# Cross attention and an MLP on one core: the second slot reordered, a transpose three steps later, the last tile's column halves in two banks

## The chip, the cores and the metric

The kernel runs on one core of a Trainium2 chip. The metric is the device time of one execution in microseconds (us), as the median of several runs. Five engines take part: TensorE (PE in the profile, with its weight loads as PEld), VectorE (DVE), ScalarE (ACT), GpSimd (POOL) and SyncE (SP), which here issues DMAs only.

## The reference, cut to what matters

There are B = 8 batches, H = 8 heads, S = 512 rows, 32 state rows and D = 64. Softmax attention runs both ways between `x` and `state`, the results of a batch are laid out as 544 rows of 512 values, and all rows go through an MLP with exact GELU and 2048 inner columns.

```python
a = softmax(scale * x @ state.T);   xread = a @ state      # 512 rows of a head
a2 = softmax(scale * state @ x.T);  sread = a2 @ x         # 32 rows of a head
rows = concatenate([xread, sread])                         # heads side by side: [B * 544, 512]
h = rows @ w_in
out = (0.5 * h * (1 + erf(h / sqrt(2)))) @ w_out           # float32
```

## The kernel before

The work is staged by batch. For a batch `b`:

- `xtr_dma` (L269) transposes its `x` by DMA into `xT`, after `rearr` (L214) on POOL has put it in order. `scores` (L316, once for each half) multiplies on PE and takes the exponent on ACT. `norm` (L338) sums, inverts and multiplies on DVE into `a`. `atr_dma` (L364) transposes `a` by DMA into `AT`, from SP's queue.
- `pmat` or `p_run` (L429, L798) makes P, the product of the state with `w_in`, in four chunks of 512 columns. A chunk takes eight small matmuls into two banks of PSUM and one copy each by ACT and DVE (`p_copy`). P lets the read-out and the first layer of the MLP be one product.
- `M(k)` is the first layer: with `k = 16 * b + m` it multiplies `P` by `AT` for the m-th 128 inner columns (L478, two matmuls) and takes the GELU on ACT (L485). Two of them, a pair, make one step of a slot.
- `U(u)` is a quarter of the second layer for one block of rows in batches 0 and 1 (`mm2`, L504, four matmuls). From batch 2 on the second layer is instead done with seven products of half-size blocks (Strassen's scheme in Winograd-like form): `g_sum` forms sums of GELU blocks on DVE (L580), `X(b, name)` multiplies them (L586) and combines the results on DVE, ACT and POOL (L605, L608, L635, L641, L643). `w_sums(i)` forms the sums of weights that this needs, on DVE (L552). `load_x` on POOL fetches a later batch, held back by a tiny copy named `hold` that waits for a GELU.
- `sread(b)` multiplies for the 32 state rows, `sread_out` normalises them, and `srt(b)` (L399) transposes them on PE into a bank of PSUM, from where DVE copies them into `XSR` (L405). `XSR` is read in the last slot only, by `mm1_sr` (L518), which handles the state rows of all batches.

The order of each engine's work is written out by hand: the schedule is manual, and each engine executes its instructions in the order in which the program issues them. A slot is the stretch with the `M` of one batch, in eight steps p = 0 to 7. The slots of batches 2 to 7 are one loop (L948), in which `X` and `g_sum` of the batch before, `scores`, `norm`, `atr_dma`, `srt` and the P chunks of the next batch have their steps. The second slot, of batch 1, is written out at its beginning (M(16) to M(19)) and is then a loop over p = 2 to 7 (L923).

PSUM has eight banks here: four with the tag `f`, which `ftile` gives out in turn to `M`, `scores`, `pmat`, `sread` and `srt`, and four with tags `o0` to `o3`, which `otile` gives out by name or in turn to the second layer and to some chunks of P. A tile in a bank can be written again only when its reader is done.

The last batch has its own tail: `L4`, `L5`, `L2`, `L1`, `L7`. `L1` and `L7` sum two products into the same bank, one after the other, for the two row blocks `j` of 128 rows and NH = 256 columns. The result of `L1` is read out with an add (L693) before `L7` adds its own product and is read with another add (L717). For j = 1 `L7` goes by column halves of 128, both in one tile, and the last DMA is issued from ACT.

Of the kernel before, what the change touches and what calls it, by code (L numbers as in the profile page):

```python
# [17 lines left out]
def kernel(  # L18
# [36 lines left out]
    def otile(shape, name, at=None):  # L55
        if at is None:
            at = turn[0] % 4
            turn[0] += 1
        return ps_o.tile(shape, FP32, name=name, tag=f"o{at}")
# [256 lines left out]
    def scores(b, half):  # L316
        A = atts[b]
        if half == 0:
            begin_e(b)
        pt = ps_f.tile([128, SJ, 2, 2, NS], FP32, name="pt", tag="f")  # L320
        for ci in range(2):
            c = 2 * half + ci
            for j in range(SJ):
                nc.tensor.matmul(  # L324
                    pt[:, j, :, ci, :],
                    lhsT=A.xT[:, j, c, :],
                    rhs=sbd[:, b, c, :],
                    start=True,
                    stop=True,
                )  # L330
        nc.scalar.activation(  # L331
            out=A.e[:, :, 64 * half:64 * half + 64],
            in_=pt.rearrange("p j t c n -> p (j t) (c n)"),
            func=AF.Exp,
            scale=scale,
        )

    def norm(b, half):  # L338
        A = atts[b]
        G = SJ * 2  # L340
        hs = slice(64 * half, 64 * half + 64)
        e4 = A.e[:, :, hs].rearrange("p g (c n) -> p g c n", n=NS)
        cs = att.tile([128, G, 2], FP32, name="cs", tag="cs")
        nc.vector.reduce_sum(out=cs, in_=e4, axis=AX.X)  # L344
        ics = att.tile([128, G, 2], FP32, name="ics", tag="ics")
        nc.vector.reciprocal(out=ics, in_=cs)
        nc.vector.tensor_tensor(  # L347
            out=A.a[:, :, hs].rearrange("p g (c n) -> p g c n", n=NS),
            in0=e4,
            in1=ics[:, :, :].to_broadcast((128, G, 2, NS)),  # L350
            op=ALU.mult,
        )
# [11 lines left out]
    def atr_dma(b):  # L364
        A = atts[b]
        A.AT = att.tile([128, SJ, 2, 128], BF16, name="AT", tag="AT")
        nc.sync.dma_start_transpose(
            out=A.AT.rearrange("p j t n -> p (j t) n"), in_=A.a
        )
# [59 lines left out]
    def pmat(b, f):  # L429
        p_copy(b, f, p_mm(b, f, ftile))  # L430
# [152 lines left out]
    def x_mm(ps, lhs, rhs, first, js=(0, 1)):  # L583
        for j in js:
            for m in range(MH):
                nc.tensor.matmul(  # L586
                    ps[:, j - js[0], :],
                    lhsT=lhs[:, m, 128 * j:128 * j + 128],
                    rhs=rhs[:, m, :],
                    start=(first and j == js[0] and m == 0),  # L590
                    stop=(m == MH - 1),
                    skip_group_check=True,
                )
# [54 lines left out]
    def rows_out(h, js, ns, eng):  # L648
        b = B - 1
        rows = out[b * SB:b * SB + S, :].rearrange("(p j) n -> p j n", j=SJ)  # L650
        eng.dma_start(
            out=rows[:, 2 * h + js.start:2 * h + js.stop, ns], in_=xs[b, "o", h][:, js, ns]
        )
# [25 lines left out]
    def L2():  # L679
# [5 lines left out]
        xs[b, "v"] = c_tile("v")  # L685
        nc.vector.tensor_tensor(out=xs[b, "v"], in0=xs[b, "y"], in1=c21, op=ALU.subtract)

    def L1():
        b = B - 1
        for j in range(2):  # L690
            ps = xs[b, "x", j] = otile([128, 1, NH], "xp", 2 - 2 * j)
            x_mm(ps, xs[b, "g1"], w_sum["1"], True, (j,))
            nc.vector.tensor_tensor(  # L693
                out=xs[b, "o", 1][:, j, right],
                in0=ps[:, 0, :],
                in1=xs[b, "v"][:, j, :],
                op=ALU.add,
            )
        rows_out(1, both, right, nc.sync)

    def L7():
        b = B - 1
        o = xs[b, "o", 0]
        h = NH // 2
        for j, pieces in ((0, ((0, NH),)), (1, ((0, h), (h, NH)))):
            ps = xs[b, "x", j]
            for n0, n1 in pieces:
                for m in range(MH):
                    nc.tensor.matmul(
                        ps[:, 0, n0:n1],  # L710
                        lhsT=xs[b, "g7"][:, m, 128 * j:128 * j + 128],
                        rhs=w_sum["7"][:, m, n0:n1],
                        start=False,
                        stop=(m == MH - 1),
                        skip_group_check=True,
                    )
                nc.vector.tensor_tensor(  # L717
                    out=o[:, j, n0:n1],
                    in0=ps[:, 0, n0:n1],
                    in1=xs[b, "u"][:, j, n0:n1],  # L720
                    op=ALU.add,
                )
                eng = nc.scalar if j and n0 else nc.sync
                rows_out(0, slice(j, j + 1), slice(n0, n1), eng)

    rs = {}

# [80 lines left out]
    def M(*ms):  # L808
        for m in ms:
            mm1(m // MC, m % MC)  # L810
# [109 lines left out]
    U(16)  # L920


    u = 17  # L923
    for p in range(2, 8):
        if p == 4:
            scores(2, 0)
            scores(2, 1)
            norm(2, 0)
            norm(2, 1)
        if p == 7:  # L930
            atr_dma(2)
        if p == 3:
            begin(3)
            rearr(3)
            xtr_dma(3)
            rearr_ones(3)
        M(16 + 2 * p, 17 + 2 * p)
        U(u)
        u += 1
        if p in (5, 7):  # L940
            pmat(2, 2 + p // 7)
        if p >= 3:
            w_sums(p - 3)
        if p == 2:
            nc.gpsimd.tensor_copy(out=hold, in_=gs[1][:, 4, 0:1])
            load_x(4)

    for b in range(2, B):  # L948
        nb = b + 1
        for p in range(8):  # L950
            k = 16 * b + 2 * p
            if p == 1 and nb < B:
                scores(nb, 0)
                scores(nb, 1)
            if p in (2, 3) and nb < B:
                norm(nb, p - 2)
            if p == 3 and nb + 1 < B:
                xtr_dma(nb + 1)
            if p == 5 and nb < B:
                atr_dma(nb)  # L960
            if p == 3 and nb < B:
                srt(b)
            if p == 7 and nb == B - 1:
                srt(nb)
            M(k, k + 1)
            if b == 2:
                for _ in range(2 if p < 4 else 1):
                    if u < 32:
                        U(u)
                        u += 1  # L970
            elif p < 5:
                if p == 0:
                    g_sum(b - 1, "5")
                X(b - 1, "45127"[p])
                if p < 3:
                    g_sum(b - 1, "127"[p])
            if nb == B and p < 4:
                for m in range(4 * p, 4 * p + 4):
                    mm1_sr(m)
            if p == 1 and nb < B:  # L980
                sread(b)
                sread_out(b)
            if p == 4 and nb == B - 1:
                sread(nb)
                sread_out(nb)
            if p == 0 and b + 3 < B:
                nc.gpsimd.tensor_copy(out=hold, in_=gs[b][:, 0, 0:1])  # L987
                load_x(b + 3)
            if p == 0 and nb + 1 < B:
                begin(nb + 1)  # L990
                rearr(nb + 1)
            if p == 2 and nb + 1 < B:
                rearr_ones(nb + 1)
            if nb == B:
                if p == 4:
                    r_homes()
                    r_sum("5")
                    r_sum("2")
                if p == 5:
                    g_sum(b, "6")  # L1000
                    R("3")
                    r_sum("1")
                    R("4")
                    r_sum("6")
                    r_sum("7")
                if p == 6:
                    R("5")
                    X(b, "3")
                    R("2")
                    R("1")  # L1010
                if p == 7:
                    R("6")
                    X(b, "6")
                continue
            if p == 5:
                g_sum(b, "6")
                if nb < B:
                    p_run(nb, (0, 1), ((0, 1), (3, 2)))
            if p == 6:
                X(b, "3")  # L1020
            if p == 7:
                if nb < B:
                    p_run(nb, (2, 3), ((1, 2), None))
                X(b, "6")
# [41 lines left out]
```

The softmax here doesn't subtract the row's maximum and nothing guards it: scores larger than these inputs give would overflow.

## Time and profile before

| What | Value |
|---|---|
| Median of 11 runs | 209.74 us (209.39 to 211.74) |
| The profiled execution | 209.43 us, span 207.7 us |
| Granted clock of TensorE | 0.997 |
| Busy in the span: PE, DVE, ACT, POOL | 97%, 66%, 64%, 30% |
| Second slot from M(20) to the first M of batch 2 | from 41.63 to 54.82 us |
| First matmul of `L7` | from 202.26 us |

The span reaches from the first instruction of the profile to the last; the profiled execution's own time is 1.7 us longer. Rows of a timeline give the start, the length, the engine, the line, the operation and its tiles, and in brackets how long the engine was idle before and what released it. Rows of waits give the engine and line that waited, what for, the total in us, how often, and the longest. The ends of matmuls are modelled, so stretches of PE's work are best taken from start to start. Starts below are in us from the beginning of the span.

### The profile page before, as it was taken

What the parts mean: (1) busy time and instruction counts of PE and PEld (TensorE: products, weight loads), DVE (VectorE), ACT (ScalarE), POOL (GpSimd) and SP (SyncE); (2) the same over time, 40 slices, a digit from 0 to 9 for tenths busy, and PEclk for the clock granted to TensorE, in tenths of its full rate; (3) what the DMA queues carried; (4) which work ended last, traced back from release to release, by engine and by line L of the source; (5) the groups of instructions that cost most, each with busy time, mean ns of one, the idle gap of its engine ahead of it and who ended that gap; (6) DMA issues with size and microseconds to landing.
All of it is one profiled execution on the core that took longest, in us unless ns stands there. A gap on an engine that the chain in (4) does not pass through costs nothing.

```text
span 207.7 us, 4699 instructions
## 1 busy us (share of the span) xinstructions
PE 200.9 (97%) x1971; PEld 131.1 (63%) x1971; DVE 137.9 (66%) x218; ACT 133.2 (64%) x240; POOL 62.4 (30%) x69
## 2 busy tenths in 40 slices
PE   7799999998999999999999999999999999999993
PEld 7545444453454577756775677667775787778882
DVE  2954675748929649994699658855887553165872
ACT  3864866679794779565956787587757576744120
POOL 8964402573171015710577005500220001200000
PEclk9999999999999999999999999999999999999998
DMA  6999999789384908736681505360106001030224
GB/s 197 198 183 204 206 193 191 149 183 186 51 101 105 251 0 103 154 141 64 72 170 60 159 0 74 88 197 3 52 3 202 3 0 51 3 152 0 54 103 152
DMA packets 40261, 23.14 MB, mean 111 GB/s; under 512 B 21808, under 2 KB 38320, under 8 KB 40240
## 3 DMA queue, kind: packets, MB, share of 16 engines
q0 software_dynamic: 13936, 8.10, 28.4%
q1 hardware_dynamic: 25616, 14.36, 27.4%
q10 hardware_dynamic: 688, 0.39, 0.6%
q8 instruction: 15, 0.25, 0.5%
q14 instruction: 6, 0.05, 0.1%
HBM read 17.30 MB, written 8.91 MB: 126 GB/s over the span
## 4 chain that ended last, share of the span: by engine, by line
PE 79%; DVE 12%; POOL 4%; ACT 3%; issue 1%; POOLq 0%; DVEq 0%; ACTq 0%
PE xp L586 28%; PE hp L478 22%; PE op L504 9%; DVE gsum L580 5%; PE p_ps L415 4%; PE op L531 3%; PE hps L518 3%; PE rp L764 3%; DVE a L347 2%; POOL w_in_bf L105 2%; DVE cs L344 1%; PE sr L378 1%; PE pt L324 1%; POOL sbd L95 1%; ACT g L485 1%
## 5 line engine op out<-in xcount | busy, mean ns | idle before, releaser
L485 ACT ACTIVATE g<-hp 128x512 bf16<-128x512 f32 x124 | 67.6, 603 | 31.6 <-PE hp L478 26.5
L478 PE MATMUL hp<-AT,P 128*128 128x512 bf16 x248 | 64.2, 380 | 0.5 <-DVE XSR L405 0.4
L586 PEld LDWEIGHTS <-gsum 128*128 128x128 bf16 x464 | 45.0, 98 | 11.5 <-issue 2.1
L580 DVE TENSOR_TENSOR gsum<-g 128x2048 bf16<-128x2048 bf16 x30 | 39.3, 1328 | 0.1
L478 PEld LDWEIGHTS <-P 128*128 128x128 bf16 x248 | 22.3, 98 | 21.2 <-issue 4.0
L586 PE MATMUL xp<-ws,gsum 128*128 128x256 bf16 x272 | 32.5, 273 | 0.0
L427 DVE CAST P<-p_ps 128x512 bf16<-128x512 f32 x31 | 20.1, 684 | 15.1 <-PE p_ps L415 15.1
L504 PE MATMUL op<-w_out_bf,g 128*128 128x512 bf16 x96 | 23.7, 379 | 0.0
L586 PE MATMUL xp<-ws,g 128*128 128x256 bf16 x192 | 22.9, 273 | 0.0
L586 PE MATMUL xp<-w_out_bf,gsum 128*128 128x256 bf16 x192 | 22.8, 273 | 0.0
L586 PEld LDWEIGHTS <-g 128*128 128x128 bf16 x192 | 18.8, 98 | 4.3
L426 ACT CAST P<-p_ps 128x512 bf16<-128x512 f32 x31 | 17.0, 604 | 6.5 <-PE p_ps L415 6.5
L635 POOL TENSOR_TENSOR u<-s,oh 128x512 f32<-128x512 f32 x5 | 6.3, 1266 | 49.0 <-ACT oh L632 49.0
L504 PEld LDWEIGHTS <-g 128*128 128x128 bf16 x96 | 9.1, 98 | 11.5 <-issue 1.1
L218 POOL COPY x<-xb 128x1024 bf16<-128x1024 bf16 x12 | 12.6, 1082 | 10.8 <-DMA xb<-in_x_dram 10.8
L228 POOL COPY xo<-xb 128x1024 bf16<-128x1024 bf16 x12 | 14.5, 1241 | 1.3 <-PE sr L378 1.3
L347 DVE TENSOR_TENSOR a<-e,ics 128x512 bf16<-128x512 bf16 x14 | 13.9, 995 | 0.5
L344 DVE TENSOR_REDUCE cs<-e 128x16 f32<-128x512 bf16 x14 | 9.5, 676 | 3.8 <-ACT e L331 3.8
L415 PE MATMUL p_ps<-w_in_bf,sbd 64*32 64x512 bf16 x248 | 11.2, 382 | 0.6 <-ACT g L485 0.5
L605 POOL TENSOR_TENSOR v<-q,oh 128x512 f32<-128x512 f32 x5 | 6.4, 1278 | 14.8 <-ACT oh L637 14.8
L629 DVE TENSOR_TENSOR s<-xp,s 128x512 f32<-128x512 f32 x5 | 3.5, 691 | 11.0 <-PE xp L586 11.0
L987 POOL COPY hold<-g 128x1 bf16<-128x1 bf16 x3 | 1.0, 329 | 31.5 <-ACT g L485 31.5
(111 smaller groups left out, 221.9 us busy)
## 6 DMA issues: line engine op xcount, KB each, us to landing
xb<-in_x_dram POOLq DMA_DIRECT2D x7, 512.0 KB, 6.5
out_dram<-oh SPq DMA_DIRECT2D x13, 256.0 KB, 2.5
out_dram<-osb SPq DMA_DIRECT2D x10, 256.0 KB, 3.3
out_dram<-oh SPq DMA_DIRECT2D x5, 512.0 KB, 2.8
w_out_bf<-in_moe_w_out_dram POOLq DMA_DIRECT2D x4, 512.0 KB, 12.5
w_in_bf<-in_moe_w_in_dram POOLq DMA_DIRECT2D x6, 256.0 KB, 11.7
x0f<-in_x_dram SPq DMA_DIRECT2D x3, 256.0 KB, 4.0
w_in_bf<-in_moe_w_in_dram POOLq DMA_DIRECT2D x4, 128.0 KB, 4.1
```

The source lines that it names most:

```text
L218: nc.gpsimd.tensor_copy(out=A.x4[:, :, :, 64 * t:64 * t + 64].rearrange("p j c d -> p c j d"), in_=src[:, t],)
L228: eng.tensor_copy(out=A.xo[:, :, :, 2 + 64 * t:66 + 64 * t].rearrange("p j c d -> p c j d"), in_=src[:, t],)
L344: nc.vector.reduce_sum(out=cs, in_=e4, axis=AX.X)
L347: nc.vector.tensor_tensor(out=A.a[:, :, hs].rearrange("p g (c n) -> p g c n", n=NS), in0=e4, in1=ics[:, :, :].to_broadcast((128, G, 2, NS) ...
L415: nc.tensor.matmul(ps[t][32 * c:32 * c + 32, :], lhsT=sbd[64 * t:64 * t + 64, b, c, 32 * t:32 * t + 32], rhs=w_in_bf[64 * t:64 * t + 64, c ...
L426: nc.scalar.copy(out=dst[:, 0, :], in_=ps[0])
L427: nc.vector.tensor_copy(out=dst[:, 1, :], in_=ps[1])
L478: nc.tensor.matmul(hp, lhsT=Ps[b][:, t, m * 128:(m + 1) * 128], rhs=atts[b].AT[:, :, t, :], start=(t == 0), stop=(t == 1),)
L485: nc.scalar.activation(out=gs[b][:, m, :], in_=hp, func=AF.Gelu)
L504: nc.tensor.matmul(ps, lhsT=gs[b][:, m, j * 128:(j + 1) * 128], rhs=w_out_bf[:, m, :], start=(m == 0), stop=(m == MC - 1),)
L580: nc.vector.tensor_tensor(out=t, in0=g_q(b, h0, k0), in1=g_q(b, h1, k1), op=op)
L586: nc.tensor.matmul(ps[:, j - js[0], :], lhsT=lhs[:, m, 128 * j:128 * j + 128], rhs=rhs[:, m, :], start=(first and j == js[0] and m == 0), ...
```

## The change

It has three parts. In the tail, `L1` and `L7` share a list of three pieces: row block 0 with 256 columns in bank `o2`, and row block 1 as two column halves of 128 in banks `o0` and `o1`. `L1` therefore makes its second row block as two sets of eight matmuls. In the loop over the slots `srt(b)` goes from step 3 to step 6. The second slot from step 2 on is written out instead of looped: chunk 2 of batch 2's P goes ahead of `M(22, 23)`, the scores of batch 2 ahead of `U(18)`, its norms behind `U(18)`, two `U` go between `M(26, 27)` and `M(28, 29)`, `U(23)` comes in from the next slot, whose loop starts with `u = 24`, and the sums of weights are placed differently.

```diff
+    PIECES = ((0, 0, NH, 2), (1, 0, NH // 2, 0), (1, NH // 2, NH, 1))
+
+    def l_mm(ps, name, j, n0, n1, first):
+        for m in range(MH):
+            nc.tensor.matmul(
+                ps,
+                lhsT=xs[B - 1, "g" + name][:, m, 128 * j:128 * j + 128],
+                rhs=w_sum[name][:, m, n0:n1],
+                start=(first and m == 0),
+                stop=(m == MH - 1),
+                skip_group_check=True,
+            )
+
     def L1():
         b = B - 1
-        for j in range(2):
-            ps = xs[b, "x", j] = otile([128, 1, NH], "xp", 2 - 2 * j)
-            x_mm(ps, xs[b, "g1"], w_sum["1"], True, (j,))
+        for j, n0, n1, at in PIECES:
+            ps = xs[b, "x", j, n0] = otile([128, n1 - n0], "xp", at)
+            l_mm(ps, "1", j, n0, n1, True)
             nc.vector.tensor_tensor(
-                out=xs[b, "o", 1][:, j, right],
-                in0=ps[:, 0, :],
-                in1=xs[b, "v"][:, j, :],
+                out=xs[b, "o", 1][:, j, NH + n0:NH + n1],
+                in0=ps,
+                in1=xs[b, "v"][:, j, n0:n1],
                 op=ALU.add,
             )
         rows_out(1, both, right, nc.sync)
 
     def L7():
         b = B - 1
-        o = xs[b, "o", 0]
-        h = NH // 2
-        for j, pieces in ((0, ((0, NH),)), (1, ((0, h), (h, NH)))):
-            ps = xs[b, "x", j]
-            for n0, n1 in pieces:
...
-                eng = nc.scalar if j and n0 else nc.sync
-                rows_out(0, slice(j, j + 1), slice(n0, n1), eng)
+        for j, n0, n1, at in PIECES:
+            ps = xs[b, "x", j, n0]
+            l_mm(ps, "7", j, n0, n1, False)
+            nc.vector.tensor_tensor(
+                out=xs[b, "o", 0][:, j, n0:n1], in0=ps, in1=xs[b, "u"][:, j, n0:n1], op=ALU.add
+            )
+            rows_out(0, slice(j, j + 1), slice(n0, n1), nc.scalar if n0 else nc.sync)
...
-    u = 17
-    for p in range(2, 8):
-        if p == 4:
-            scores(2, 0)
-            scores(2, 1)
-            norm(2, 0)
-            norm(2, 1)
-        if p == 7:
-            atr_dma(2)
-        if p == 3:
-            begin(3)
-            rearr(3)
-            xtr_dma(3)
-            rearr_ones(3)
-        M(16 + 2 * p, 17 + 2 * p)
-        U(u)
-        u += 1
-        if p in (5, 7):
-            pmat(2, 2 + p // 7)
-        if p >= 3:
-            w_sums(p - 3)
-        if p == 2:
-            nc.gpsimd.tensor_copy(out=hold, in_=gs[1][:, 4, 0:1])
-            load_x(4)
-
+    M(20, 21)
+    U(17)
+    nc.gpsimd.tensor_copy(out=hold, in_=gs[1][:, 4, 0:1])
+    load_x(4)
+    w_sums(0)
+    pmat(2, 2)
+    begin(3)
+    rearr(3)
+    xtr_dma(3)
+    rearr_ones(3)
+    M(22, 23)
+    scores(2, 0)
+    scores(2, 1)
+    U(18)
+    norm(2, 0)
+    norm(2, 1)
+    M(24, 25)
+    U(19)
+    M(26, 27)
+    U(20, 21)
+    w_sums(1)
+    M(28, 29)
+    w_sums(2)
+    U(22)
+    atr_dma(2)
+    M(30, 31)
+    U(23)
+    pmat(2, 3)
+    w_sums(3)
+    w_sums(4)
+
+    u = 24
     for b in range(2, B):
...
-            if p == 3 and nb < B:
+            if p == 6 and nb < B:
                 srt(b)
```

More of the change, by code (lines that the diff above doesn't have):

```diff
@@ L702, in L7 @@
         b = B - 1
-        o = xs[b, "o", 0]
-        h = NH // 2
-        for j, pieces in ((0, ((0, NH),)), (1, ((0, h), (h, NH)))):
-            ps = xs[b, "x", j]
-            for n0, n1 in pieces:
[L708 to L722, printed above, removed]
-                eng = nc.scalar if j and n0 else nc.sync
-                rows_out(0, slice(j, j + 1), slice(n0, n1), eng)
+        for j, n0, n1, at in PIECES:
[5 more added lines that the diff above has]
+            rows_out(0, slice(j, j + 1), slice(n0, n1), nc.scalar if n0 else nc.sync)
     rs = {}
```

## The prediction

> **What bounds the kernel now.** I read the page first: busy times and the chain that ended last.
>
> ```profile
> PE 200.9 (97%) x1971; PEld 131.1 (63%) x1971; DVE 137.9 (66%) x218; ACT 133.2 (64%) x240; POOL 62.4 (30%) x69
> PE 79%; DVE 12%; POOL 4%; ACT 3%; issue 1%; POOLq 0%; DVEq 0%; ACTq 0%
> ```
>
> TensorE (PE) is the bound. The change takes no arithmetic away from it, so all it can win is idle time inside PE's order. The view of waits, for PE alone, names the three places that it touches:
>
> ```profile
> PE p_ps L415 <- ACT g L485: 0.5, 1, 0.5
> PE xp L709 <- DVE oh L717: 0.4, 1, 0.4
> PE hp L478 <- DVE XSR L405: 0.4, 2, 0.2
> ```
>
> The ends of matmuls are modelled[...], so these figures are too small. I size each place by the starts in the timeline instead. Costs of PE work, as differences of starts: a pair of `M` 0.86 us, one `U` 0.86, two `scores` 0.47, a chunk of P 0.44 (0.34 and the change of shape around it), one `X` 1.75.
>
> Second slot, timeline of all engines:
>
> ```profile
> 45.56 1.28 ACT L331 ACT_TABLE_LOAD   x1 [0.49 <-PE pt L324]
> 46.85 1.08 ACT L331 ACTIVATE e<-pt 128x512 bf16<-128x512 f32 x2
> 47.95 1.28 ACT L485 ACT_TABLE_LOAD   x1
> 49.25 2.06 ACT L485 ACTIVATE g<-hp 128x512 bf16<-128x512 f32 x4
> 49.90 0.89 PE L415 MATMUL p_ps<-w_in_bf,sbd 64*32 64x512 bf16 x8 [0.46 <-ACT g L485]
> 50.85 1.93 SPq L367 DMA_TRANSPOSE AT<-a  x1
> ```
>
> ACT leaves the gelus for 3.7 us. The `f` tag has four banks, taken in turn, so PE can go only four tiles ahead. From `M(20)` (41.63) to `M(32)` (54.82) are 13.19 us. The work in it is six pairs of `M` 5.18, six `U` 5.18, scores 0.47, two chunks of P 0.88: 11.71. **Idle: 1.48 us.**
>
> Slot of batch 3, steps 3 to 5:
>
> ```profile
> 88.16 1.26 DVE L347 TENSOR_TENSOR a<-e,ics 128x512 bf16<-128x512 bf16 x1
> 89.34 0.71 DVE L405 COPY XSR<-srT 128x128 bf16<-128x128 bf16 x1
> 89.68 0.89 DVE L608 TENSOR_TENSOR oh<-xp,v 128x512 f32<-128x512 f32 x1
> 90.11 0.59 PE L478 MATMUL hp<-AT,P 128*128 128x512 bf16 x2 [0.17 <-DVE XSR L405]
> 90.49 0.68 DVE L643 TENSOR_TENSOR oh<-xp,u 128x512 f32<-128x512 f32 x1
> 91.22 0.10 PEld L415 LDWEIGHTS <-sbd 64*32 64x32 bf16 x6 [0.47 <-issue]
> ```
>
> DVE has no gap from 78.12 to here. PE waits first for the copy of `srt`, then, inside the chunks of P, for the bank that L643 empties. From `M(58)` (89.35) to `M(60)` (91.56) are 2.21 us; the same steps in batch 2 (67.91 to 69.42) take 1.51. **Lost: 0.70**; in batch 4 (111.49 to 113.75) 0.75. Batches 2, 5 and 6 show no wait there.
>
> Tail:
>
> ```profile
> 202.26 1.48 PE L709 MATMUL xp<-ws,gsum 128*128 128x256 bf16 x16
> 203.34 0.74 DVE L717 TENSOR_TENSOR oh<-xp,u 128x256 f32<-128x256 f32 x2 [0.45 <-PE xp L709]
> 204.13 0.61 PE L709 MATMUL xp<-ws,gsum 128*128 128x128 bf16 x8 [0.38 <-DVE oh L717]
> 204.77 0.29 DVE L717 TENSOR_TENSOR oh<-xp,u 128x128 f32<-128x128 f32 x1 [0.70 <-PE xp L709]
> 205.09 0.37 ACTq L651 DMA_DIRECT2D out_dram<-oh  x1
> ```
>
> The last eight matmuls wait for the read of the other half of their bank: 203.57 to 204.13, **0.56 us**.
>
> **Part 1, the second slot.** Same instructions, other order; `U(23)` comes in from the next slot (0.86). PE's new order from 41.63: `M(20,21)` `U(17)` to 43.36, P chunk to 43.80, `M(22,23)` to 44.66, scores to 45.13, `U(18)` 45.99, `M(24,25)` 46.86, `U(19)` 47.72, `M(26,27)` 48.59, two `U` 50.31, `M(28,29)`, `U`, `M(30,31)`, `U`, P chunk, `M(32)` at 54.20 if nothing waits. ACT: gelus of 20, 21 until 43.34; cast of P 43.92 to 44.51 (it starts 0.47 behind the chunk, as at 54.48 and 54.95); gelus of 22, 23 until 45.60; table load to 46.88; exps end 47.42 and 47.96; table load to 49.24; gelus 24 to 27 at 49.79, 50.33, 50.87, 51.41. The banks in turn: `M(26)` needs the first exp (47.42, wanted 47.72), `M(27)` the second (47.96, wanted 48.15), `M(28)` gelu 24 (49.79, wanted 50.31), `M(29)` gelu 25 (50.33, wanted 50.74). All four come in time, by 0.2 to 0.5. ACT's absence is unmoved; before it stand now a chunk of P with its banks already free, and behind it two `U` in place of one. So all 1.48 goes, if both switches cost what this row shows.
>
> A rule speaks against it. The row: the load takes 1.28 and the first exp starts at 46.85, 0.01 after it. The Trainium skill (ScalarE: Activation LUTs, "What ACT_TABLE_LOAD costs") gives each switch a drain of about 1.38 besides, 2.66 in all. With it the first exp would end at 48.80 and gelu 24 at 52.55; `M(26)` would be 1.1 late and `M(28)` again 1.05, and the whole sum at the end would be about 0.5 us. I take the row, which has no such gap at either switch.
>
> What is late next: `AT` of batch 2. The norms hang on the exps, which end as before, so its DMA again starts at 50.85 and lands 3.2 later (the one such issue in that stretch), 54.05. `M(32)` wants it at 54.20 instead of 54.82. Bounds 0 to 1.7 (the slowest `AT` takes 5.1); I take 0. SP still sees `xT` (46.61, held by POOL's `rearr`, unmoved) ahead of `AT`, and no output between. POOL's order is unchanged: hold, `load_x(4)`, `rearr`, `rearr_ones`. On DVE `w_sums(0)` ends (43.8) before the moved cast is ready; the other weight sums fall behind the norms and are first used 15 us later.
>
> Removing a `U` from step 4 of batch 2 leaves `M(40)` to `M(43)` in a row there: 1.73 of PE against 2.16 of gelus. From `M(40)` at 65.52 (66.18 before, less 0.62 and the moved `srt`) ACT ends them at 68.31, its cast of the first chunk at 68.85; `X(2,"3")` takes that bank at 68.67. With the restart I book **0.25** lost (bounds 0 and 0.5). Part 1: 1.48 - 0.25 = 1.23.
>
> **Part 2, `srt` at step 6.** One transpose (0.06) and a 0.72 copy move. On DVE L608 then follows `a` directly: 89.36 to 90.05, L643 to 90.66 instead of 91.17. `M(59)` no longer waits, and the second chunk restarts 0.5 earlier. The remainder (0.2 to 0.25) stays, since L643 is still later than the 90.53 at which PE wants its bank. Gain **0.48** in batch 3, and the same reckoning in batch 4 (L643 112.85 instead of 113.36); 0 elsewhere: 0.96. Bounds 0 and 1.45.
>
> At step 6 the copy goes behind both casts of P on DVE, and the fourth `f` tile later, the second `M` of step 7, wants its bank. Batch 3: casts end 93.0, copy 93.75, wanted 94.2. The margin is 0.45 there, 0.25 to 1.0 elsewhere (batch 6 the smallest); DVE's next demand, the casts of the later chunks, waited 2.15 to 2.38 us for PE in batches 2, 3 and 5, so the copy fits into that. In batch 6 `srt(6)` and `srt(7)` are both ahead of the read of XSR (165.82).
>
> **Part 3, the tail.** `L1` now takes its second row half as 16 matmuls 128 wide. The row: eight such take 0.61 with a tail of 0.17, so 0.44, as the eight of 256 take 0.87: nothing is added. The skill (Perfetto Trace Analysis, "Matmuls") says that larger matmuls are more efficient where possible. If each of the eight added weight loads cost its full 98 ns, that would be 0.78 and the part a loss of 0.2; but the 128-wide row loads seven in 0.43, beside the matmuls. The adds of `L1` grow from two of 0.42 to 0.42 and two of 0.29, done by 202.77, and the banks' next users come at 202.26 (bank 2, read by 202.0), 203.13 and 203.57. `L7` then runs through: last matmul issued by 204.01, add 204.21 to 204.50, DMA from ACT at 204.53 instead of 205.09. SP's half is issued by about 204.6, lands no later. Gain **0.56** (bounds 0.4 and 0.65).
>
> **Sum:** 1.23 + 0.96 + 0.56 = 2.75, say 2.7. The profiled execution took 209.43 (span 207.7 and 1.7 around it): 206.7. The median shown is 0.31 above it: **207.0**. About 0.3% (0.63 us) is what a measurement can tell from no change.
>
> **Rivals.**
> A: the second slot still waits, at `M(32)` for `AT`, or at the exps' banks. For it: margins of 0.15 to 0.5 us. Against: every duration in that order has a row. If 1.3 of 1.48 is lost the sum is 1.4: 208.3.
> B: `srt` brings nothing, since L608 and L643 wait for POOL's `v` and for `X` anyway. For it: in batches 5 and 6 L608 idles 0.5 to 0.6 for `v`. Against: in batch 3 `v` ends at 88.87, before L608 could start. Gain 1.8: 207.9.
> C, on the other side: the moved copy blocks PE. Place: the second `M` of step 7, five slots. Price: the lateness, and about 0.3 for the restart. It decides once the copy ends 0.9 us later than I put it in every slot: then 0.45 + 0.3 each is lost, 3.75 in all, which gives 210.7. Against: only 0.25 to 1.0 of margin is reckoned, but the rows ahead of it (casts 1.28) are steady.
> That the halves don't part is hardly possible: they become two tiles in two banks.
>
> **How the numbers follow.** Forecast 0.68, A 0.14, B 0.08, C 0.06; 0.04 that smaller waits eat up everything. Faster 0.90, within 0.3% 0.04, slower 0.06. Low end: every wait gone, 1.48 + 1.45 + 0.65 = 3.6, so 206.1. High end: a little beyond A, 208.5.
>
> **What would show it.** Right: no PE wait on ACT in the second slot, `M(32)` near 54.2 with `U(23)` done; the stretch `M(58)` to `M(60)` 1.7 to 1.75 long; no wait for L717 in the tail, last DMA 0.55 earlier against the last `X`. Wrong: PE waiting at `M(32)`, or `hp` in step 7 waiting for XSR, or gelus after the second table load starting later than 49.3.

## The result, and the profile after

The changed kernel takes 206.91 us as the median of 12 runs (206.30 to 207.66), against 209.71 for the kernel before in the runs beside it: a ratio of 0.9859, with a 95% interval from 0.9841 to 0.9877. The two medians differ by 2.8 us, where 2.7 was forecast. The ratio is taken over all runs and not from the two medians, whose own quotient is 0.987; by it the change saves about 3.0 us (2.6 to 3.3). The span of the profiled execution, which took 206.66 us, is 204.9 us instead of 207.7.

The page of the kernel after, its busy times and the chain that ended last:

```profile
PE 198.6 (97%) x1979; PEld 130.5 (64%) x1979; DVE 138.0 (67%) x219; ACT 132.8 (65%) x240; POOL 62.3 (30%) x69
PE 92%; DMA 4%; POOL 2%; DVE 0%; issue 0%; POOLq 0%
```

The share of DVE in the chain fell from 12% to nothing: from 13.73 us, where the load of `w_out` has landed, to the last add of the tail at 201.99, the chain now follows PE's own order alone. The view of waits for PE after says the same. All that it lists lies in the first twelve microseconds, which the change doesn't touch (after the engine and line: what was waited for, total us, times, longest):

```profile
PE warm_ps L146 <- DVE warm L92: 1.0, 1, 1.0
PE aT_ps L361 <- POOL a L309: 0.9, 1, 0.9
PE xT_ps L250 <- ACT x0b L236: 0.5, 1, 0.5
PE st_ps L173 <- ACT st_bf L169: 0.3, 1, 0.3
PE pc L285 <- DVE xT L254: 0.2, 1, 0.2
```

The second slot after, from the timeline of all engines:

```profile
41.95 1.03 PE L478 MATMUL hp<-AT,P 128*128 128x512 bf16 x4
45.86 1.28 ACT L331 ACT_TABLE_LOAD   x1
47.15 1.09 ACT L331 ACTIVATE e<-pt 128x512 bf16<-128x512 f32 x2
48.26 1.28 ACT L485 ACT_TABLE_LOAD   x1
49.55 3.05 ACT L485 ACTIVATE g<-hp 128x512 bf16<-128x512 f32 x6
51.15 1.24 SPq L367 DMA_TRANSPOSE AT<-a  x1
54.52 0.55 PEld L478 LDWEIGHTS <-P 128*128 128x128 bf16 x4 [0.23 <-DMA AT<-a]
54.52 1.04 PE L478 MATMUL hp<-AT,P 128*128 128x512 bf16 x4
```

ACT leaves the gelus for the same 3.7 us, and PE doesn't notice. From `M(20)` to `M(32)` are 12.57 us with `U(23)` inside, exactly the work that the prediction counted. The 0.23 ahead of the last weight load is the usual change of shape after a chunk of P; before the change the same 0.23 stood there. `AT` was issued at 51.15 and landed 3.1 later, at 54.25, so it had about 0.3 of room in this execution.

Batch 3, steps 3 to 6, the same view:

```profile
87.00 1.20 DVE L347 TENSOR_TENSOR a<-e,ics 128x512 bf16<-128x512 bf16 x1
88.12 0.68 DVE L608 TENSOR_TENSOR oh<-xp,v 128x512 f32<-128x512 f32 x1
88.14 1.03 PE L478 MATMUL hp<-AT,P 128*128 128x512 bf16 x4
88.72 0.67 DVE L643 TENSOR_TENSOR oh<-xp,u 128x512 f32<-128x512 f32 x1
89.09 0.77 PE L415 MATMUL p_ps<-w_in_bf,sbd 64*32 64x512 bf16 x16
89.79 0.23 PE L402 MATMUL srT<-ident,srm 128*128 128x128 bf16 x1
89.86 1.03 PE L478 MATMUL hp<-AT,P 128*128 128x512 bf16 x4
91.65 0.71 DVE L405 COPY XSR<-srT 128x128 bf16<-128x128 bf16 x1
```

The read-outs L608 and L643 follow the norm directly, and the pair at 88.14 runs in one piece. What is left of the wait is in the chunks' 0.77, where 0.62 is usual.

The tail:

```profile
198.25 3.70 PE L692 MATMUL xp<-ws,gsum 128*128 128x256 bf16 x48
201.09 0.74 DVE L719 TENSOR_TENSOR oh<-xp,u 128x256 f32<-128x256 f32 x2 [0.58 <-PE xp L692]
201.99 0.29 DVE L719 TENSOR_TENSOR oh<-xp,u 128x128 f32<-128x128 f32 x1 [0.15 <-PE xp L692]
202.31 0.36 ACTq L651 DMA_DIRECT2D out_dram<-oh  x1
```

All 48 matmuls of `L1` and `L7` are one unbroken row, and the last DMA is issued 4.06 us after the first of them, instead of 4.57.

Measured from start to start, the whole difference is found. The third column adds 0.06 to each of the two middle rows for `srt`'s transpose, which now lies inside the stretch and no longer ahead of it.

| Stretch | Before, us | After, us | Saved |
|---|---|---|---|
| `M(20)` to `X(2,"3")` | 28.66 | 27.19 | 1.47 |
| `M(58)` to `M(60)` | 2.21 | 1.72 | 0.55 |
| `M(74)` to `M(76)` | 2.26 | 1.77 | 0.55 |
| first matmul of `L1` to the last DMA's issue | 4.57 | 4.06 | 0.51 |

The starts before, for the first two rows and the last, and that of `X(2,"3")` after:

```profile
41.63 1.03 PE L478 MATMUL hp<-AT,P 128*128 128x512 bf16 x4
54.82 1.04 PE L478 MATMUL hp<-AT,P 128*128 128x512 bf16 x4
70.29 1.91 PE L586 MATMUL xp<-ws,g 128*128 128x256 bf16 x16
89.35 0.59 PE L478 MATMUL hp<-AT,P 128*128 128x512 bf16 x2
91.56 1.04 PE L478 MATMUL hp<-AT,P 128*128 128x512 bf16 x4
200.52 1.91 PE L586 MATMUL xp<-ws,gsum 128*128 128x256 bf16 x16
```

```profile
69.14 1.91 PE L586 MATMUL xp<-ws,g 128*128 128x256 bf16 x16
```

The savings add up to 3.08. The profiled execution after reached `M(20)` 0.32 later (41.95 instead of 41.63). The change touches nothing ahead of `M(20)`, and its start varies from run to run: another execution of the same kernel reached it at 41.51, and others of kernels with the same beginning between 41.87 and 43.12. 3.08 less 0.32 is 2.76, of the 2.8 by which the spans differ.

### The profile page after: what moved, and what is told of

Same layout as the page of the kernel before. It is cut to its first block, busy times and chain, and to the rows that moved or that the text cites. A ratio compares the mean times of both kernels' runs of the same rounds, so it can differ in the third digit from the quotient of the medians.

```text
span 204.9 us, 4716 instructions
## 1 busy us (share of the span) xinstructions
PE 198.6 (97%) x1979; PEld 130.5 (64%) x1979; DVE 138.0 (67%) x219; ACT 132.8 (65%) x240; POOL 62.3 (30%) x69
## 4 chain that ended last, share of the span: by engine, by line
PE 92%; DMA 4%; POOL 2%; DVE 0%; issue 0%; POOLq 0%
PE xp L586 34%; PE hp L478 27%; PE op L504 10%; PE p_ps L415 4%; DMA w_out_bf<-in_moe_w_out_dram 4%; PE op L531 4%; PE hps L518 3%; PE rp L762 3%; PE xp L692 2%; PE pt L324 2%; PE sr L378 1%; POOL w_in_bf L105 1%; POOL sbd L95 1%; PE srT L402 1%; PE xT_ps L264 0%; PE aT_ps L361 0%
## 5 line engine op out<-in xcount | busy, mean ns | idle before, releaser
L586 PEld LDWEIGHTS <-gsum 128*128 128x128 bf16 x448 | 43.4, 98 | 11.3 <-issue 2.1
L580 DVE TENSOR_TENSOR gsum<-g 128x2048 bf16<-128x2048 bf16 x30 | 39.8, 1347 | 0.1
L586 PE MATMUL xp<-ws,gsum 128*128 128x256 bf16 x256 | 30.6, 273 | 0.0
L415 PE MATMUL p_ps<-w_in_bf,sbd 64*32 64x512 bf16 x248 | 10.3, 382 | 0.0
```

The source lines that it names most:

```text
L415: nc.tensor.matmul(ps[t][32 * c:32 * c + 32, :], lhsT=sbd[64 * t:64 * t + 64, b, c, 32 * t:32 * t + 32], rhs=w_in_bf[64 * t:64 * t + 64, c ...
L580: nc.vector.tensor_tensor(out=t, in0=g_q(b, h0, k0), in1=g_q(b, h1, k1), op=op)
L586: nc.tensor.matmul(ps[:, j - js[0], :], lhsT=lhs[:, m, 128 * j:128 * j + 128], rhs=rhs[:, m, :], start=(first and j == js[0] and m == 0), ...
```

## The experiments

**Each part alone.** Three kernels, each with one part of the diff of the change and the rest as before: the written-out second slot with `u = 24`; `if p == 6` for `srt`; the list of pieces in `L1` and `L7`. Ratios are again over all runs.

> The second slot's new order alone. Theory (each part's gain stands by itself): 1.45 us off, so about 208.3 and a ratio of 0.993; M(20) to M(32) takes 12.57 with U(23) inside, no wait of PE on ACT in it; X(2,"3") follows M(45) at once or with at most 0.1 lost. Rival (the 0.25 that the prediction booked at X(2,"3") is real, and was hidden in the full change by the moved transpose): 1.2 off, 208.5, with a gap ahead of X(2,"3").

> The move of srt to step 6 alone. Theory: M(58) to M(60) takes 1.72 instead of 2.21 and M(74) to M(76) 1.77 instead of 2.26, so 0.98 off, about 208.75 and a ratio of 0.9953; batches 2, 5 and 6 gain nothing. Rival (the read-outs in those steps wait for POOL's v or for X anyway, and the gain seen in the full change comes from the earlier start): under 0.3 off, 209.4 or more.

> The two banks for the column halves alone. Theory: the wait for the first half's read goes, the stretch from the first matmul of L1 to the last DMA's issue shrinks from 4.57 to 4.06, so 0.5 off, about 209.2 and a ratio of 0.9976. Rival (the end is set by the DMAs that SP issues, or the added weight loads cost their full 98 ns each): within 0.2 of no change, or slower.

| Kernel | Ratio to before | 95% interval | What the trace shows |
|---|---|---|---|
| slot alone | 0.9937 | 0.9908 to 0.9967 | `M(20)` to `M(32)` 12.57; `X(2,"3")` right behind `M(45)`, 0.14 lost ahead of the chunk of P before it |
| `srt` alone | 0.9958 | 0.9937 to 0.9978 | the two stretches 1.73 and 1.78 |
| tail alone | 0.9966 | 0.9939 to 0.9992 | first matmul of `L1` to the last DMA's issue 4.06 |

The product of the three ratios is 0.9862, the ratio of the whole change 0.9859: within their intervals the parts add up. The traces show one small exception, the 0.14 of the first row. In that kernel DVE's copies out of the second layer's banks (L491) stand behind `srt`'s copy and end at 67.70, and the chunk of P starts at 67.76; with `srt` moved they end at 67.25 and nothing is lost. So the slot alone saves 1.34 up to `X(2,"3")`, and 1.47 together with the move of `srt`.

The rival of `srt` falls by trace and by time. The slot's rival falls by the trace alone, which has no gap ahead of `X`; the time cannot tell 1.2 from 1.45 us. The tail's rival falls by the trace as well: from the issue of the last DMA to the end of the span are 2.56 to 2.58 us before, after and with the tail alone, so the 0.51 reaches the end. Its time alone would not settle it, since the interval reaches 0.9992. The loss that the prediction booked at `X(2,"3")` is at most that 0.14, and it is not at `X`.

**Which of the slot's moves does it.** The five kernels from here on, up to the one with three copies, ran once each. Their times are set against the 206.66 us of the full change's profiled execution, in which `M(20)` started at 41.95. In each of the five, the later start of `M(20)` and what the stretches lost account for the time to 0.02 us. In the first kernel the chunk of P goes back behind the two `U`. In the second the chunk stays ahead, but one `U` stands at each place as before.

```diff
     w_sums(0)
-    pmat(2, 2)
...
     U(20, 21)
+    pmat(2, 2)
```

> The full change, with the chunk 2 of P back behind M(26,27) and the two U. Theory (four banks in turn; what makes up for ACT's absence is the second U and not the chunk's place): M(28) and M(29) then want the banks of gelus 26 and 27, which come 0.05 to 0.15 late, so M(20) to M(32) takes 12.6 to 12.8 instead of 12.57. Rival (the chunk ahead is what removes the stall): most of the 1.48 comes back, 13.5 or more.

`M(20)` to `M(32)` took 12.72 us, 0.15 more than in the full change. The time was 206.93 us, with `M(20)` 0.10 later. With two `U` in place, the chunk's place is worth only 0.15; the rival is out.

```diff
-    U(20, 21)
+    U(20)
...
-    U(22)
+    U(21)
...
-    U(23)
+    U(22)
...
-    u = 24
+    u = 23
```

> The full change, with one U at each place as before, so U(20) alone stands between M(26,27) and M(28,29), and the loop starts with u = 23. Theory (four banks in turn): M(28) waits for gelu 24 and M(29) for gelu 25, 0.4 to 0.5 in all, so M(20) to M(32), which now holds one U less (11.71 of work), takes 12.1 to 12.3; the end moves by about 0.45, to 207.35. Rival (the chunk ahead is enough by itself): 11.75, and no change in time.

It took 207.99 us (`M(20)` 0.11 later), and `M(20)` to `M(32)` 12.92, against 11.71 of work: 1.21 lost, more than either theory allowed. The timeline of this kernel shows two pieces:

```profile
47.04 4.65 SPq L271 DMA_TRANSPOSE xT<-x  x1
50.30 1.08 PE L478 MATMUL hp<-AT,P 128*128 128x512 bf16 x4 [0.27 <-ACT g L485]
51.79 1.25 SPq L367 DMA_TRANSPOSE AT<-a  x1
54.98 0.55 PEld L478 LDWEIGHTS <-P 128*128 128x128 bf16 x4 [0.96 <-DMA AT<-a]
54.98 1.04 PE L478 MATMUL hp<-AT,P 128*128 128x512 bf16 x4 [0.67 <-ACT P L426]
```

`M(28)` waits for a gelu, and by starts this costs 0.43 ahead of the pair and 0.05 inside it, 0.48 as reckoned. The other 0.73 is at `M(32)`. The two rows at 54.98 name different causes, and the weight load's is the one that fits: `AT` was issued at 51.79 and needs 3.1, which gives 54.89, while the chunk's cast has nothing that `M(32)` reads. `AT` was late because SP was still issuing `xT` until 51.69; `a` had been ready since about 51.2. So this kernel tells two things: without the second `U` the banks keep PE waiting for 0.48, and `AT` is the next bound.

Since either move alone leaves so little, a last kernel has neither: the chunk goes behind `U(20)`, and one `U` stands at each place. Of the slot's moves hardly more is left than the scores ahead of `U(18)`.

```diff
     w_sums(0)
-    pmat(2, 2)
...
-    U(20, 21)
+    U(20)
+    pmat(2, 2)
...
-    U(22)
+    U(21)
...
-    U(23)
+    U(22)
...
-    u = 24
+    u = 23
```

> The full change, with the chunk of P back behind U(20) and one U at each place (the loop starts with u = 23), so that of the slot's moves hardly more than the scores ahead of U(18) is left. Theory (the moves cover in turn for the same absence of ACT, each where the banks let PE go on): the chunk waits for the banks of gelus 24 and 25, M(28) and M(29) for those of 26 and 27, about 1.0 in all of the 1.48 from before; M(20) to M(32) is 12.75, with 11.71 of work in it. Rival (the scores' place does it all): 11.75 to 11.9. Second rival (it does nothing): 13.2.

`M(20)` to `M(32)` took 12.73 us, so 1.02 of the 1.48 is back, as reckoned. The time of 208.63 us holds a start of `M(20)` that was 0.96 later than in the full change, ahead of everything that was edited. In its timeline the chunk waits as it did before the change:

```profile
50.72 0.90 PE L415 MATMUL p_ps<-w_in_bf,sbd 64*32 64x512 bf16 x8 [0.48 <-ACT g L485]
51.69 1.08 PE L478 MATMUL hp<-AT,P 128*128 128x512 bf16 x4
```

By what the banks still cost, the moves rank so: from 1.48 the scores' place takes it to 1.02; the chunk ahead besides to 0.48, or the second `U` besides to 0.15; both to 0.

**How near that bound is.** One sum of weights goes between the two norms on DVE.

```diff
     norm(2, 0)
+    w_sums(1)
     norm(2, 1)
...
     U(20, 21)
-    w_sums(1)
```

> The full change, with one sum of weights (1.22 of DVE) put between the two norms of batch 2. Theory (AT of batch 2 is the next thing to be late, with 0.2 to 0.3 of room): its DMA is issued 1.2 later and M(32) waits for it, 0.9 to 1.1 later than now, all of which reaches the end: about 207.9. Rival (the DMA lands earlier than reckoned, and there is room): M(32) at 12.57 behind M(20), 206.9.

The timeline of this kernel:

```profile
52.25 1.23 SPq L367 DMA_TRANSPOSE AT<-a  x1
55.37 0.55 PEld L478 LDWEIGHTS <-P 128*128 128x128 bf16 x4 [1.11 <-DMA AT<-a]
```

`M(32)` came 13.45 behind `M(20)`, 0.88 later than in the full change, with `AT` issued 1.13 later in the same measure. The room was about 0.25 against the full change's profiled execution. The time was 207.51, 0.85 more; 0.9 to 1.1 had been expected.

That room is not the same in every execution. `AT` was issued 9.20 us behind `M(20)` in the full change's first profile and 9.19 in one of the later copy of `xo` below, but 9.38 to 9.40 in three others with the same slot (the slot alone, the full change again, the later copy of `xo` the first time). There SP was still issuing `xT`, although `a` was ready. `M(32)` came 3.12 to 3.19 behind the issue of `AT` in the three kernels in which it waited for it, so 12.57 leaves hardly 0.1 of room in those executions. In the kernel of the next experiment, whose slot is the same, `AT` came 9.58 behind `M(20)` and cost 0.17.

**The moved copy's room.** The prediction's rival C had the copy of `srt` block PE at the second `M` of step 7. Here the copy is made three times over.

```diff
-        nc.vector.tensor_copy(out=XSR[:, :, :, b], in_=ps)
+        for _ in range(copies):
+            nc.vector.tensor_copy(out=XSR[:, :, :, b], in_=ps)
...
-                srt(b)
+                srt(b, 3)
```

> The full change, with the copy of the moved transpose made three times over (two more of about 0.65 on DVE at step 6 of batches 2 to 6), which puts to the test the rival C of the prediction. Theory (the copy has 0.4 to 1.0 of room before the fourth tile after it wants its bank): in batches 3 and 4 the second M of step 7 comes 0.7 to 1.0 later, less in 2, 5 and 6, 2 to 3.5 in all: 209 to 210.5. Rival (DVE has over 1.5 of idle time there, so nothing waits): 206.9 to 207.2.

It took 209.33 us. Batches 3 and 4 in the timeline of this kernel:

```profile
92.38 2.24 DVE L406 COPY XSR<-srT 128x128 bf16<-128x128 bf16 x3
93.19 1.03 PE L479 MATMUL hp<-AT,P 128*128 128x512 bf16 x4
94.15 0.93 PE L416 MATMUL p_ps<-w_in_bf,sbd 64*32 64x512 bf16 x16
95.01 1.92 PE L587 MATMUL xp<-ws,gsum 128*128 128x256 bf16 x16
114.94 2.24 DVE L406 COPY XSR<-srT 128x128 bf16<-128x128 bf16 x3
117.23 0.41 PE L416 MATMUL p_ps<-w_in_bf,sbd 64*32 64x512 bf16 x7 [0.54 <-DVE XSR L406]
```

Both `M` of step 7 run at 93.19 without a stop, while the copies last until 94.62. The wait is behind them, in the last chunk of P: in batch 4 its last seven matmuls start at 117.23, just after the copies end at 117.18, and the trace names the copies as the cause. The bank numbers in the built program agree: the bank of `srt` goes to the second tile of that chunk, the sixth with the tag `f` behind it and not the fourth. From the step 7 chunks to `X` the five slots lost 0, 0.30, 0.92, 0.17 and 0.52, 1.91 in all. (This execution was also 0.57 later at `M(20)`, and lost 0.17 to `AT` at `M(32)`; with these its span is accounted for.) The size is near the lower end of what the theory expected, its place is wrong, and the rival's "nothing waits" is wrong as well.

**The rest of the wait in the chunks of P.** POOL copies `xo` while DVE does the norm at step 2, as the full change's timeline shows in batch 3:

```profile
82.53 2.48 POOL L228 COPY xo<-xb 128x1024 bf16<-128x1024 bf16 x2
82.55 1.56 DVE L347 TENSOR_TENSOR a<-e,ics 128x512 bf16<-128x512 bf16 x1
```

The full change with that copy two steps later:

```diff
-            if p == 2 and nb + 1 < B:
+            if p == 4 and nb + 1 < B:
                 rearr_ones(nb + 1)
```

> The full change, with rearr_ones of the batch after next on POOL at step 4 instead of step 2. Theory (what is left of the wait in the P chunks of batches 3 and 4, 0.15 and 0.20, is DVE's lateness, and that comes from norms stretched from 0.69 to 1.56 while POOL copies): the norm at step 2 goes back to about 0.7, the read-outs end 0.4 earlier, and 0.3 to 0.35 goes, about 206.55. Rival (POOL's copy now stretches the sums and casts that follow, or delays POOL's v or u): no gain or a loss, 206.9 to 207.3.

Batch 3 in the timeline of this kernel:

```profile
82.52 0.69 DVE L347 TENSOR_TENSOR a<-e,ics 128x512 bf16<-128x512 bf16 x1
85.86 0.69 DVE L347 TENSOR_TENSOR a<-e,ics 128x512 bf16<-128x512 bf16 x1
87.62 2.02 POOL L228 COPY xo<-xb 128x1024 bf16<-128x1024 bf16 x2
87.71 0.69 DVE L608 TENSOR_TENSOR oh<-xp,v 128x512 f32<-128x512 f32 x1 [1.16 <-POOL v L605]
88.92 1.80 DVE L580 TENSOR_TENSOR gsum<-g 128x2048 bf16<-128x2048 bf16 x1
89.07 0.63 PE L415 MATMUL p_ps<-w_in_bf,sbd 64*32 64x512 bf16 x16
```

The norm took 0.69 instead of 1.56, the chunks 0.63 instead of 0.77, and both stretches are 1.58 long where the full change has 1.72 and 1.77: 0.33 saved, as expected. The sum of gelus at 88.92 now overlaps POOL's copy and takes 1.80 instead of 1.21; it has room. The read-out L608 now waits 1.16 for POOL's `v`, and PE does not wait for it. The median of six runs was 207.17 us, not the 206.55 expected, and the ratio to before 0.9839 (0.9807 to 0.9872), too near to that of the full change to tell apart. The two ran together once more.

> The full change once more, on the same chip as the next run, so that the two can be compared. Theory: the ratio to the kernel before is 0.986 again, about 206.9. Rival: none of substance; it is the measure for the next run.

> The full change with rearr_ones at step 4, once more. Theory (its trace shows 0.33 less in the two P chunks than the full change's, and nothing lost elsewhere): 0.3 to 0.35 under the full change on the same chip, a ratio to the kernel before of about 0.9845. Rival (what the trace of one execution shows is lost again in others): no difference to the full change.

On that chip the full change had 0.9826 (0.9792 to 0.9861), 206.56 us, and this kernel 0.9806 (0.9776 to 0.9836), 206.32 us. The difference of 0.24 us has the sign and about the size of the trace's 0.33 (here again 1.59 against 1.72 in batch 3), but the intervals overlap: the gain in the stretches is shown, the gain in time is likely.

## Why the prediction was right

**Second slot.** Right to the hundredth: 1.48 was counted as idle, and 12.57 us remained. The drain that the Trainium skill adds to each table load (ScalarE: Activation LUTs, "What ACT_TABLE_LOAD costs") would have left over 2 us of waiting; at both switches the next activation again starts 0.01 behind the 1.28 of the load. It was right to take the row. Taking nothing for `AT` was in part luck. The prediction had SP issue `xT` ahead of it as before and gave that no cost. In the run the issue of `xT` took 4.10 us instead of 3.17 and ended at 51.04, just as `a` became ready (51.09). Had it taken a little longer, as in the kernel with three copies (4.50), `AT` would have been late.

**The 0.25 booked at `X(2,"3")`.** This term was mis-sized. It measured 0 in the full change and at most 0.14 with the slot alone. From `M(40)` the prediction had ACT's first cast end after 3.33 us and `X` want the bank after 3.15. In the run `X` started after 3.31 with nothing waited for, because the change of shape ahead of the chunk and `srt`'s transpose, 0.16 together, had been left out of PE's side; and on ACT's side the four gelus took 2.06, not 2.16, so that the first cast had ended after 3.18.

**`srt`.** 0.96 forecast. The two stretches got shorter by 0.49 each, 0.98, though `srt`'s transpose now lies inside them; with its 0.06 each the gain is 1.10. That a remainder would stay at L643's bank was right; it measured 0.14 and 0.19, judged by the kernel that removes it. What made L643 late, the norm that runs beside POOL's copy, the prediction had not looked for.

**The tail.** 0.56 forecast, 0.51 measured. The eight added weight loads cost nothing that can be seen: 48 of them in 3.63 us, beside the matmuls. The Trainium skill's preference for larger matmuls (Perfetto Trace Analysis, "Matmuls") had no price here.

**Sum.** 2.75 was forecast, and the stretches sum to 3.08: 0.25 more in the slot, where nothing was lost at `X`, 0.14 more from `srt` and 0.05 less in the tail. That the spans differ by 2.8 all the same comes from the start of that one execution, 0.32 later. So the mechanism and each part hold, and that the sum agrees to a tenth of a microsecond is luck.

**The rivals.** A did not come true, but it was the nearest: `AT` had 0.25 to 0.3 of room in one profile of the full change and hardly 0.1 in the other, and three of the experiments used it up. B fell with the `srt` kernel. C named a wrong place: "the second `M` of step 7" rested on the assumption that the banks of the `f` tag go round in turn. In the second slot they do; around `srt` they don't, and the copy has the room until the last chunk of P. That PE waited in the second slot where the reckoning by four banks in turn put it, in three kernels, bears the slot's part out.

## What to carry to other kernels

When an engine must leave the main path for a fixed time, count how much work its consumer has that needs none of the shared buffers, and put enough of it behind the gap: here one more group of four matmuls behind it left 0.15 us of the wait, while a moved operation ahead of it left 0.48. When a stall is removed, name what comes next and how far off it is, down to the queue that issues it: here the room in front of a DMA went from 0.3 us to less than nothing with the time that the queue spent on the transfer ahead of it. And read which buffer a tile really gets before costing a wait on it.

## What the runs showed of the hardware

- A multiplication on DVE with both inputs in SBUF was stretched from 0.69 to 1.56 us while POOL copied in SBUF, and the sum of gelus from 1.21 to 1.80; the read-outs with one input in PSUM stayed at 0.67 to 0.69. This fits the Trainium skill (SBUF — State Buffer, "Who interferes with whom"), which has a DVE instruction with two SBUF inputs contend with a POOL instruction that reads SBUF.
- SP needed 3.0 to 3.2 us to issue the DMA of `xT` in the five kernels whose P chunk stands late in the second slot, and 4.1 to 4.65 in the eight executions with the chunk ahead. Nothing that feeds this DMA was moved, and it starts 5.0 us behind `M(20)` in either kind. It matters, since `AT` is issued behind it. In all thirteen traces the issue ends within about 0.3 us of the landing of `xb`, which `load_x(4)` on POOL started 2.9 us before `xT`; that load landed 6.0 to 6.4 us after its issue with the chunk late and 7.3 to 7.8 with the chunk ahead. The two delays go together. What causes them was not tried and stays open.
